# Keeping B11 + T2 apart, left operands stored one by one, half of x added by the stores, and 320 bytes in the constants

## The chip, the core and the metric

The kernel runs on one core of one Trainium2 chip. The metric is the device time of one execution in microseconds, the median of several. A profile of one further execution shows every engine: TensorE (PE) multiplies, VectorE (DVE), ScalarE (ACT) and GpSimd (POOL) work on elements, SyncE (SP) issues most transfers, POOL issues others. Sixteen DMA engines carry them all.

## What is computed

x has 2048 rows of 1024, normalised row by row to xn. One branch is linear attention with 32 heads of 32, the other a gated MLP with 3584 hidden columns; the output is x + s * silu(...). Cut to what matters:

```
xn = layernorm(x)
q, k, v = split(xn @ wqkv)                       # 32 heads of 32
s = attention(phi(q), phi(k), v) @ wo            # linear attention, first part's rest
h = silu(xn @ w1) * (xn @ w3)                    # 2048 x 3584
out = x + s * silu(h @ w2)
```

All is float32.

## The kernel before

Every large product is done by a scheme with seven products in place of eight. Two matrices are cut into 2x2 blocks; the left side gives the operands A11, A12, A22 and the sums S1 to S4, the right side B11, B21, B22 and the sums T1 to T4. The seven products are named after the right operand: B11 (with A11), T2 (S2), T3 (S3), T1 (S1), B21 (A12), T4 (A22), B22 (S4). With U = B11 + T2 the four result blocks are c11 = B11 + B21, c12 = U + T1 + B22, c21 = U + T3 + T4 and c22 = U + T3 + T1. A block A21 is needed for the sums alone. Each float32 operand is split into a high and a low half ("split", lines 82 to 84: a cast on ScalarE, a subtraction on VectorE), and each product of halves is three matmuls of 128 x 128 by 512 columns (lines 91 to 93).

The first part (to about 1700 us) makes q, k, v and the hidden h, in two halves of the rows. `hidden` (line 604) multiplies gate and up and writes h to DRAM as h_d (line 616, issued by POOL); `four_sums` lets POOL form S1 to S4, which are written as hs_d (line 624, POOL in the first half, mostly SP in the second). `divide` does the same for q and writes qs_d (line 750). The buffers of h ("sg", four) and of the sums (a pool of six) come free when the store has read them.

The second part is a row of segments (class `Segment`): attention's product with the merged wo (names ending in s), then B0 (two blocks of the hidden columns deep) and B1 to B4 (three deep). Each goes through eight groups m of 256 rows. For a group `left` (line 943) loads seven left operands (line 958, into the four sg buffers; names like rA11B), `operands` splits them one group ahead, and `tokens` (line 868) does the products and the sums. A group of three blocks is 7 x 3 x 3 = 63 matmuls.

`tokens` has two forms. The inner form (from line 908) does one product after the other in four banks a to d; catch_up lets one step of other work in between. In a segment that isn't the first, the accumulators acc[m] already hold the sums of the segments before: ScalarE copies B11 to u (911), VectorE adds T2 to u (914), and POOL then adds u to c22, c21 and c12 (917 to 919), before VectorE adds the products to them (921 to 939). The outer form (from line 881) is used in the first group of a segment and the last: all seven banks are open and k is the outer loop, so that the next segment's right operands can take the place of this one's block by block. Its sums are lines 886 to 904, with four adds on POOL (894, 897, 899, 900).

In the last segment B4 every finished block goes to `finish` (line 1006): SP loads s and x (1009, 1010), ScalarE applies silu (1011), VectorE multiplies by s and adds x (1012, 1013), POOL issues the store (1014).

A scheduler of the language orders each engine's instructions by its own model of times; engines then run in order and wait for each other by semaphores. All large tiles lie in pools behind the constants, so the constants' size sets the address of every one of them.

Of the kernel before, what the change touches and what calls it, by code (L numbers as in the profile page):

```python
# [22 lines left out]
def tile_linear_attention_times_swiglu(  # L23
# [706 lines left out]
    def divide(m, k):  # L730
# [13 lines left out]
        def steps(t):  # L744
# [5 lines left out]
            nc.gpsimd.dma_start(out=qs_d[m][:, k], in_=t)  # L750
# [87 lines left out]
    class Segment:  # L838


        def __init__(self, name, nk, first, place, right, left, acc, end=None):
# [23 lines left out]
        def add(self, e, dst, src, fresh=False):  # L865
            e.tensor_add(out=dst, in0=src, in1=dst)

        def tokens(self, m, outer, between):
# [3 lines left out]
            u = pe.tile([P, C], F32, tag="u", name=f"u{name}")  # L872
# [6 lines left out]

            if outer:  # L880
# [5 lines left out]
                nc.scalar.copy(out=u, in_=b["B11"])  # L886
                if self.first:
                    V.tensor_add(out=c11, in0=b["B21"], in1=u)
                    V.tensor_add(out=u, in0=b["T2"], in1=u)
                    V.tensor_add(out=c21, in0=b["T3"], in1=u)  # L890
                    V.tensor_add(out=c12, in0=b["T1"], in1=u)
                    V.tensor_add(out=c22, in0=b["T1"], in1=c21)
# [208 lines left out]
```

## Time and profile before

| | us |
|---|---|
| median of 3 runs | 2417.58 |
| lowest, highest | 2417.55, 2421.8 |
| profiled execution, own time | 2424.34 |
| its span, first to last instruction | 2422.6 |
| PE busy | 2343.7 (97%) |
| DVE busy | 1804.7 (74%) |
| ACT busy | 934.6 (39%) |
| POOL busy | 723.7 (30%) |
| moved by DMA | 408.62 MB |

The span is the time between the first and the last instruction of the profiled execution. Busy shares are means over stages with different limits; a stage is read by windows of time. A wait names the instruction that came last, by its engine, tile and line.

### The profile page before, as it was taken

Reading aid. Unit: us, or ns where it says so; the run is one execution under the profiler, and the core shown is the slowest. Engines: PE = TensorE matmul, PEld = TensorE weight load, DVE = VectorE, ACT = ScalarE, POOL = GpSimd, SP = SyncE. Lnnn points to the kernel's source line nnn. Section 1 sums busy time; section 2 is a strip of 40 time slices with the busy share of each in tenths; the row PEclk is TensorE's granted clock in tenths of the full one; section 3 lists DMA queues with packets and bytes.
Section 4 is the critical chain, followed back from the end, with each engine's and each line's share of the span. In section 5 each row is a group of like instructions: output and inputs, shape, how many; then the busy total and the mean of one; then the engine's idle time right before and its main releaser. Section 6 shows DMA issues by size and latency. Waiting matters only on the chain.

```text
span 2422.6 us, 30793 instructions
## 1 busy us (share of the span) xinstructions
PE 2343.7 (97%) x10544; PEld 1932.8 (80%) x10544; DVE 1804.7 (74%) x2688; ACT 934.6 (39%) x1667; POOL 723.7 (30%) x909
## 2 busy tenths in 40 slices
PE   6999999999999999999999999999899999999997
PEld 5788888777788878888878888888687887777776
DVE  8655888888787665567877887887656777776797
ACT  4434644333232234345333323334323434343443
POOL 3000112247567210000424443234330042323253
PEclk9999999999999999999999999999999999999999
DMA  3211455566567661134455555457876545453597
GB/s 125 85 52 62 152 168 167 170 199 229 198 229 238 214 228 37 51 105 139 155 187 187 198 193 188 146 185 241 252 239 200 148 124 162 119 164 114 170 289 242
DMA packets 375133, 408.62 MB, mean 169 GB/s; under 512 B 19840, under 2 KB 308608, under 8 KB 374976
## 3 DMA queue, kind: packets, MB, share of 16 engines
q1 hardware_dynamic: 348800, 319.35, 42.4%
q0 software_dynamic: 26176, 87.31, 9.6%
q8 instruction: 82, 1.34, 0.2%
q14 instruction: 75, 0.61, 0.1%
HBM read 268.96 MB, written 137.63 MB: 168 GB/s over the span
## 4 chain that ended last, share of the span: by engine, by line
PE 49%; DVE 6%; DMA 5%; issue 3%; ACT 1%; POOL 1%; DVEq 0%; SPq 0%; POOLq 0%; ACTq 0%
PE dB L91 1%; PE dB L93 1%; PE dB L92 1%; PE cB L91 1%; PE cB L93 1%; PE cB L92 1%; PE aB L93 1%; PE aB L91 1%; PE aB L92 1%; DMA rA11B<-h_d 1%; PE den L715 1%; PE kv L508 1%; DMA wpr<-wp_d 1%; PE bB L93 1%; PE bB L92 1%
## 5 line engine op out<-in xcount | busy, mean ns | idle before, releaser
L616 POOL DMA_DIRECT2D h_d<-sg x112 | 61.5, 550 | 355.5 <-DVE sg L615 352.0
L577 POOL DMA_DIRECT2D pq_d<-pq x32 | 17.5, 545 | 487.3 <-DVE pq L469 476.3
L917 POOL TENSOR_TENSOR acc<-acc,uB 128x512 f32<-128x512 f32 x25 | 41.9, 1676 | 157.9 <-DVE uB L914 157.9
L598 POOL TENSOR_TENSOR qd<-qd 128x128 f32<-128x128 f32 x32 | 25.0, 782 | 140.5 <-DVE qd L747 118.9
L894 POOL TENSOR_TENSOR acc<-acc,uB 128x512 f32<-128x512 f32 x7 | 12.0, 1710 | 145.9 <-ACT uB L886 145.9
L602 POOL TENSOR_TENSOR hs<-sg,hs 128x256 f32<-128x256 f32 x56 | 53.2, 950 | 1.5
L630 POOL TENSOR_TENSOR w<-w 128x256 f32<-128x256 f32 x28 | 26.7, 952 | 72.5 <-DMA w<-in_B_w 61.1
L1004 POOL DMA_DIRECT2D s_d<-s x32 | 17.4, 544 | 92.4 <-DVE s L924 24.5
L599 POOL TENSOR_TENSOR hs<-hs,sg 128x256 f32<-128x256 f32 x56 | 42.7, 762 | 0.0
L598 POOL TENSOR_TENSOR hs<-sg,sg 128x256 f32<-128x256 f32 x56 | 42.1, 752 | 1.0
L601 POOL TENSOR_TENSOR hs<-sg 128x256 f32<-128x256 f32 x56 | 41.9, 749 | 0.0
L91 PE MATMUL cB<-T,XA22B 128*128 128x512 f32 x87 | 35.0, 402 | 6.3 <-DVE acc L921 5.9
L83 ACT CAST XS4B<-rS4B 128x384 fp32r<-128x384 f32 (+1 forms) x40 | 19.6, 490 | 54.5 <-PE cB L93 45.9
L919 POOL TENSOR_TENSOR acc<-acc,uB 128x512 f32<-128x512 f32 x25 | 40.1, 1605 | 0.0
L84 DVE TENSOR_TENSOR XS1B<-rS1B,XS1B 128x384 fp32r<-128x384 f32 (+1 forms) x40 | 36.6, 916 | 3.7 <-ACT XS1B L83 3.6
L935 DVE TENSOR_TENSOR acc<-cB,acc 128x512 f32<-128x512 f32 x25 | 17.2, 689 | 29.6 <-PE cB L93 29.6
L83 ACT CAST XS1B<-rS1B 128x384 fp32r<-128x384 f32 (+1 forms) x40 | 19.7, 493 | 46.8 <-PE cB L93 26.5
L1011 ACT ACTIVATE acc<-acc 128x512 f32<-128x512 f32 x32 | 20.2, 633 | 43.7 <-DVE acc L924 14.8
L91 PE MATMUL aB<-B,XA12B 128*128 128x512 f32 x87 | 34.1, 392 | 2.2 <-ACT uB L911 1.6
L83 ACT CAST XS3B<-rS3B 128x384 fp32r<-128x384 f32 (+1 forms) x40 | 19.6, 491 | 43.0 <-PE bB L93 15.6
L83 ACT CAST XA11B<-rA11B 128x384 fp32r<-128x384 f32 (+1 forms) x40 | 19.7, 492 | 41.8 <-PE dB L93 28.4
L91 PE MATMUL dB<-B,XS4B 128*128 128x512 f32 x87 | 34.4, 395 | 1.2 <-DVE acc L924 1.2
(5853 smaller groups left out, 8886.9 us busy)
## 6 DMA issues: line engine op xcount, KB each, us to landing
h_d<-sg POOLq DMA_DIRECT2D x112, 256.0 KB, 3.2
qs_d<-qd POOLq DMA_DIRECT2D x32, 512.0 KB, 3.7
hs_d<-hs POOLq DMA_DIRECT2D x60, 256.0 KB, 3.9
w<-in_B_w SPq DMA_DIRECT2D x56, 256.0 KB
wt_d<-w SPq DMA_DIRECT2D x28, 512.0 KB
hs_d<-hs SPq DMA_DIRECT2D x52, 256.0 KB
pq_d<-pq POOLq DMA_DIRECT2D x32, 256.0 KB, 3.3
a_dS<-xo SPq DMA_DIRECT2D x16, 512.0 KB
```

Source lines behind the costliest of these rows:

```text
L83: nc.scalar.copy(out=hi, in_=src)
L84: return nc.vector.tensor_sub(out=lo, in0=src, in1=hi.bitcast(F32))
L91: nc.tensor.matmul(acc, lhsT=wh, rhs=ah, start=start, stop=False, skip_group_check=True)
L92: nc.tensor.matmul(acc, lhsT=wh, rhs=al, start=False, stop=False, skip_group_check=True)
L93: nc.tensor.matmul(acc, lhsT=wl, rhs=ah, start=False, stop=stop, skip_group_check=True)
L598: nc.gpsimd.tensor_add(out=s1, in0=a21, in1=a22)
L599: nc.gpsimd.tensor_sub(out=s2, in0=s1, in1=a11)
L601: nc.gpsimd.tensor_sub(out=s3, in0=a11, in1=a21)
L602: nc.gpsimd.tensor_sub(out=s4, in0=a12, in1=s2)
L616: nc.gpsimd.dma_start(out=h_d[i][2 * h + c][:, 2 * k + n], in_=sg[n, c])
L917: G.tensor_add(out=c22, in0=c22, in1=u)
L919: G.tensor_add(out=c12, in0=c12, in1=u)
```

## The change

- u is no longer added to three accumulators in each segment. It is stored to DRAM (u_d, one tile per group, issued by POOL: `keep`), loaded again by SP in the next segment with the group's left operands, and B11 and T2 of all segments are added to it, on VectorE. Only the last segment adds it to c22, c21 (inner form: VectorE) and c12 (POOL), by `close`. In B0, which has nothing to add to yet, ScalarE copies the first product into an accumulator.
- h_d, hs_d and qs_d become stores with a place for each left operand, so that a load of one operand is one run per partition (1.5 KB for three blocks, 1 KB for B0, 2 KB for q) where it was runs of 512 bytes; the stores are cut into runs of 512 bytes. A21 isn't stored.
- In groups 0 to 6 of the last segment, the blocks of the second 128 rows don't load x and don't add it: the output's rows get x by a copy in DRAM during segment B2 (`lay_x`), and the store adds to them (`accum_op`).
- An unused constant of 80 floats per partition moves all pools behind it by 320 bytes.

```diff
+    const.tile([P, 80], F32, name="gap")
...
+    LEFT = ["A11", "A12", "A22", "S1", "S2", "S3", "S4"]
+    PLACE = {"A11": (0, 1), "A12": (2, 4), "A22": (3, 5), "S1": (6, 7), "S2": (8, 9), "S3": (10, 11), "S4": (12, 13)}
+    h_d = [[dram.tile([P, 7 * NT, (f1 - f0) // 2, P], F32, name=f"h_d{f0}_{c}") for c in range(NCH)] for f0, f1 in FB]
...
+    qs_d = [dram.tile([P, 7, ND // 2, P], F32, name=f"qs_d{m}") for m in range(S // (2 * P))]
+    u_d = [dram.tile([P, C], F32, name=f"u_d{m}") for m in range(S // (2 * P))]
...
-            nc.gpsimd.dma_start(out=h_d[i][2 * h + c][:, 2 * k + n], in_=sg[n, c])
+            src = sg[n, c].rearrange("p (g t s) -> p g t s", t=2, s=P)[:, :, 0] if n == 0 else \
+                sg[n, c].rearrange("p (e s) -> p e s", s=P)
+            nc.gpsimd.dma_start(out=h_d[i][2 * h + c][:, 2 * n:4 * n + 2, k], in_=src)
...
-                queue.dma_start(out=hs_d[i][2 * h + c][:, k, e], in_=o[e])
+                queue.dma_start(out=h_d[i][2 * h + c][:, 6 + 4 * e:10 + 4 * e, k],
+                                in_=o[e].rearrange("p (e s) -> p e s", s=P))
...
-            nc.gpsimd.dma_start(out=qs_d[m][:, k], in_=t)
+            t = t.rearrange("p e (n s) -> p (e n) s", s=P)
+            nc.gpsimd.dma_start(out=qs_d[m][:, 0, k], in_=t[:, 0])
+            nc.gpsimd.dma_start(out=qs_d[m][:, 1:, k], in_=t[:, 2:])
...
+            if not self.first:
+                self.U[m] = pe.tile([P, C], F32, tag="u", name=f"u{self.name}_{m}")
+                nc.sync.dma_start(out=self.U[m], in_=u_d[m])
...
+            def more(c, src):
+                return V.tensor_add(out=c, in0=src, in1=c)
+            def take(c, src):
+                if not self.first:
+                    return more(c, src)
+                if self.last:
+                    return V.tensor_add(out=c, in0=src, in1=u)
+                return nc.scalar.copy(out=c, in_=src)
+            def close(e, c):
+                if self.last and not self.first:
+                    e.tensor_add(out=c, in0=c, in1=u)
+            def keep():
+                if not self.last:
+                    G.dma_start(out=u_d[m], in_=u)
...
-                copied = nc.scalar.copy(out=u, in_=ba)
+                copied = nc.scalar.copy(out=u, in_=ba) if self.first else more(u, ba)
...
-                added = V.tensor_add(out=u, in0=bb, in1=u)
+                added = more(u, bb)
+                keep()
...
-                if not self.first:
-                    G.tensor_add(out=c22, in0=c22, in1=u)
-                    G.tensor_add(out=c21, in0=c21, in1=u)
-                    G.tensor_add(out=c12, in0=c12, in1=u)
...
-                added = V.tensor_add(out=c22, in0=bd, in1=c22)
+                added = more(c22, bd)
+                close(V, c22)
...
+                added = take(c21, bc)
+                close(V, c21)
                 end(1, 0)
+                close(G, c12)
...
+    ADDED = NG - 1
+    def added_by_dma(m, t):
+        return m < ADDED and t == 1
...
+            nc.gpsimd.dma_start(out=out[r0:r0 + P, cols], in_=a, accum_op=ALU.add)
+    def lay_x(m):
+        for t in range(2):
+            if added_by_dma(m, t):
+                rows = slice((2 * m + t) * P, (2 * m + t + 1) * P)
+                with tc.issue_after(loads[-1].ins):
+                    nc.sync.dma_start(out=out[rows, :], in_=x[rows, :])
```

VectorE in B4, from the end of group 5 into group 6 (uB is u, cB and dB are banks with a product, acc the accumulators, XS3B and the like the low halves of group 7's left operands), before:

```order
L914 TENSOR_TENSOR uB_6_19885<-bB_6_19887,uB_6_19885 128x512
L84 TENSOR_TENSOR XS3B_7_19862<-rS3B_7_19860,XS3B_7_19862 128x384
L1013 TENSOR_TENSOR acc_15090<-acc_15090,xs_01_19842 128x512
L84 TENSOR_TENSOR XS1B_7_19867<-rS1B_7_19865,XS1B_7_19867 128x384
L921 TENSOR_TENSOR acc_15091<-cB_6_19888,acc_15091 128x512
L924 TENSOR_TENSOR acc_15091<-dB_6_19889,acc_15091 128x512
L84 TENSOR_TENSOR XA12B_7_19872<-rA12B_7_19870,XA12B_7_19872 128x384
L1012 TENSOR_TENSOR acc_15091<-acc_15091,ss_11_19934 128x512
L931 TENSOR_TENSOR acc_15091<-aB_6_19886,acc_15091 128x512
L1013 TENSOR_TENSOR acc_15091<-acc_15091,xs_11_19933 128x512
```

After:

```order
L894 TENSOR_TENSOR uB_6_19704<-bB_6_19882,uB_6_19704 128x512
L89 TENSOR_TENSOR XS3B_7_19858<-rS3B_7_19856,XS3B_7_19858 128x384
L1043 TENSOR_TENSOR acc_15112<-acc_15112,xs_01_19838 128x512
L894 TENSOR_TENSOR acc_15113<-cB_6_19883,acc_15113 128x512
L89 TENSOR_TENSOR XS1B_7_19863<-rS1B_7_19861,XS1B_7_19863 128x384
L894 TENSOR_TENSOR acc_15113<-dB_6_19884,acc_15113 128x512
L89 TENSOR_TENSOR XA12B_7_19868<-rA12B_7_19866,XA12B_7_19868 128x384
L907 TENSOR_TENSOR acc_15113<-acc_15113,uB_6_19704 128x512
L894 TENSOR_TENSOR acc_15113<-aB_6_19881,acc_15113 128x512
L1041 TENSOR_TENSOR acc_15113<-acc_15113,ss_11_19926 128x512
```

The add of u to c22 (L907) has come to VectorE behind the add of T1, and the add of x to that block is gone.

VectorE where B2's last group and B3's first meet (T_2 and B_2 are the low halves of B3's third block of right operands), before:

```order
L898 TENSOR_TENSOR uB_7_17733<-T3B_7_17736,uB_7_17733 128x512
L901 TENSOR_TENSOR acc_15092<-T1B_7_17737,acc_15092 128x512
L84 TENSOR_TENSOR B_2_17931<-rB21B_2_17929,B_2_17931 128x512
L84 TENSOR_TENSOR T_2_17936<-rT4B_2_17934,T_2_17936 128x512
L84 TENSOR_TENSOR XA22B_0_17789<-rA22B_0_17787,XA22B_0_17789 128x384
L84 TENSOR_TENSOR B_2_17941<-rB22B_2_17939,B_2_17941 128x512
L84 TENSOR_TENSOR XS4B_0_17794<-rS4B_0_17792,XS4B_0_17794 128x384
L84 TENSOR_TENSOR XA11B_1_17958<-rA11B_1_17956,XA11B_1_17958 128x384
L904 TENSOR_TENSOR acc_15092<-B22B_7_17740,acc_15092 128x512
L903 TENSOR_TENSOR acc_15092<-T4B_7_17739,acc_15092 128x512
```

After:

```order
L894 TENSOR_TENSOR acc_15114<-T1B_7_17765,acc_15114 128x512 x2
L89 TENSOR_TENSOR B_2_17961<-rB21B_2_17959,B_2_17961 128x512
L894 TENSOR_TENSOR acc_15114<-T4B_7_17767,acc_15114 128x512
L89 TENSOR_TENSOR T_2_17966<-rT4B_2_17964,T_2_17966 128x512
L89 TENSOR_TENSOR XA22B_0_17819<-rA22B_0_17817,XA22B_0_17819 128x384
L89 TENSOR_TENSOR B_2_17971<-rB22B_2_17969,B_2_17971 128x512
L89 TENSOR_TENSOR XS4B_0_17824<-rS4B_0_17822,XS4B_0_17824 128x384
L894 TENSOR_TENSOR uB_0_17790<-B11B_0_18022,uB_0_17790 128x512
L894 TENSOR_TENSOR acc_15107<-B11B_0_18022,acc_15107 128x512
L89 TENSOR_TENSOR XA11B_1_17989<-rA11B_1_17987,XA11B_1_17989 128x384
```

Both adds of T1 now stand together, T4's add comes earlier, and two adds of the new segment's B11 stand between the low halves.

POOL at the first hidden stores of the first half (sg is h, hs its sums), before:

```order
L616 DMA h_d_0_84<-sg_0_10_2774 128x512
L598 TENSOR_TENSOR hs_0_0_0_2947<-sg_0_00_2731,sg_0_10_2774 128x256
L601 TENSOR_TENSOR hs_0_0_1_2948<-sg_0_00_2731 128x256
L624 DMA hs_d_1_105<-hs_0_1_0_2914 128x512
L602 TENSOR_TENSOR hs_0_1_1_2915<-sg_0_11_2714,hs_0_1_0_2914 128x256
```

After:

```order
L624 DMA h_d_0_85<-sg_0_10_2763 128x4x128
L603 TENSOR_TENSOR hs_0_0_0_2936<-sg_0_00_2720,sg_0_10_2763 128x256
L606 TENSOR_TENSOR hs_0_0_1_2937<-sg_0_00_2720 128x256
L632 DMA h_d_1_86<-hs_0_1_0_2903 128x4x128
L607 TENSOR_TENSOR hs_0_1_1_2904<-sg_0_11_2703,hs_0_1_0_2903 128x256
```

The order is the same; each store has four pieces per partition (two for the half without A21).

## Rows read from the trace of the kernel before

**Rows 1.** The page: span, then PE's busy time and instructions.

```profile
span 2422.6 us, 30793 instructions
PE 2343.7 (97%) x10544; PEld 1932.8 (80%) x10544; DVE 1804.7 (74%) x2688; ACT 934.6 (39%) x1667; POOL 723.7 (30%) x909
```

**Rows 2.** PE's waits: who waited, for whom: total us, times, longest.

```profile
PE cB L91 <- DVE acc L921: 5.9, 6, 1.7
...
PE cs L91 <- DVE s L921: 5.1, 1, 5.1
...
PE T4B L91 <- ACT uB L886: 3.3, 3, 1.3
```

**Rows 3.** Windows: length, busy us of each engine (instructions), PEclk, DMA share, GB/s.

```profile
600.00:700.00 100.00, 96.72 (x427) 79.79 (x426) 79.90 (x93) 29.95 (x51) 60.12 (x78) 1.00 0.61 203
...
1690.00:1730.00 40.00, 32.02 (x122) 23.94 (x121) 28.47 (x37) 15.06 (x26) 12.49 (x21) 0.91 0.78 250
1845.00:1876.00 31.00, 26.27 (x106) 19.14 (x105) 24.67 (x47) 18.07 (x37) 1.08 (x2) 0.99 0.84 255
1900.00:2000.00 100.00, 100.00 (x443) 82.81 (x442) 73.73 (x123) 39.01 (x79) 24.55 (x16) 1.00 0.48 141
2050.00:2077.00 27.00, 24.21 (x103) 18.66 (x103) 24.98 (x36) 11.38 (x22) 13.28 (x10) 1.00 0.63 186
2170.00:2195.00 25.00, 21.98 (x94) 16.89 (x92) 22.49 (x33) 9.36 (x19) 12.13 (x9) 1.00 0.61 180
2288.00:2306.00 18.00, 16.00 (x68) 12.29 (x67) 17.83 (x25) 7.64 (x15) 8.27 (x6) 1.00 0.66 199
2306.00:2409.00 103.00, 96.97 (x416) 77.02 (x414) 96.40 (x146) 39.37 (x77) 52.23 (x51) 1.00 0.91 293
2409.00:2422.60 13.60, 0.06 (x1) 0.00 (x0) 4.40 (x7) 1.26 (x2) 1.62 (x3) 0.59 0.27 99
```

**Rows 4.** Timeline in B4: start us, duration us, engine, line, operation, tiles.

```profile
2386.39 0.69 DVE L1012 TENSOR_TENSOR acc<-acc,ss 128x512 f32<-128x512 f32 x1
...
2387.00 0.69 DVE L914 TENSOR_TENSOR uB<-bB,uB 128x512 f32<-128x512 f32 x1
...
2387.60 0.55 DVE L84 TENSOR_TENSOR XS3B<-rS3B,XS3B 128x384 fp32r<-128x384 f32 x1
2387.77 1.53 POOL L917 TENSOR_TENSOR acc<-acc,uB 128x512 f32<-128x512 f32 x1 [0.93 <-DVE uB L914]
...
2388.06 1.78 DVE L1013 TENSOR_TENSOR acc<-acc,xs 128x512 f32<-128x512 f32 x1
...
2389.77 1.64 DVE L84 TENSOR_TENSOR XS1B<-rS1B,XS1B 128x384 fp32r<-128x384 f32 x1
...
2391.34 0.68 DVE L921 TENSOR_TENSOR acc<-cB,acc 128x512 f32<-128x512 f32 x1
```

**Rows 5.** POOL's groups: count, busy us, mean ns, idle before and releaser.

```profile
L616 POOL DMA_DIRECT2D h_d<-sg x112 | 61.5, 550 | 355.5 <-DVE sg L615 352.0 <-DVE c21u__6706 L453 3.5
...
L917 POOL TENSOR_TENSOR acc<-acc,uB 128x512 f32<-128x512 f32 x25 | 41.9, 1676 | 157.9 <-DVE uB L914 157.9
L919 POOL TENSOR_TENSOR acc<-acc,uB 128x512 f32<-128x512 f32 x25 | 40.1, 1605 | 0.0
L918 POOL TENSOR_TENSOR acc<-acc,uB 128x512 f32<-128x512 f32 x25 | 34.3, 1373 | 0.0
...
L724 POOL DMA_DIRECT2D r_d<-r x4 | 2.0, 512 | 56.2 <-DVE r L723 56.2
```

**Rows 6.** VectorE's groups from 1870 to 2410, same columns.

```profile
L84 DVE TENSOR_TENSOR T<-rT4B,T 128x512 fp32r<-128x512 f32 x12 | 11.5, 956 | 0.0
...
L84 DVE TENSOR_TENSOR T<-rT2B,T 128x512 fp32r<-128x512 f32 x11 | 7.5, 686 | 4.9 <-ACT T L83 4.9
```

**Rows 7.** Chain that ended last: start us, us, what (here transfers).

```profile
1697.16 7.24 DMA rA11q<-qs_d
...
1716.06 7.71 DMA rS3q<-qs_d
...
2376.71 3.54 DMA rA11B<-h_d
```

More of the change, by code (lines that the diff above doesn't have):

```diff
@@ L838, in tile_linear_attention_times_swiglu, with __init__ @@
     class Segment:
-        def __init__(self, name, nk, first, place, right, left, acc, end=None):
+        def __init__(self, name, nk, first, last, place, right, left, acc, end=None):
+            self.last, self.U = last, {}
             self.name, self.nk, self.first = name, nk, first
@@ L871, in tokens @@
             c11, c12, c21, c22 = (self.acc(m, t, n) for t in range(2) for n in range(2))
-            u = pe.tile([P, C], F32, tag="u", name=f"u{name}")
+            u = pe.tile([P, C], F32, tag="u", name=f"u{name}") if self.first else self.U[m]
             ks = range(self.nk)
@@ L885, in tokens @@
                     between(k)
-                nc.scalar.copy(out=u, in_=b["B11"])
                 if self.first:
+                    nc.scalar.copy(out=u, in_=b["B11"])
                     V.tensor_add(out=c11, in0=b["B21"], in1=u)
[L889 to L892, printed above, removed]
-                else:
-                    G.tensor_add(out=c11, in0=c11, in1=u)
-                    V.tensor_add(out=c11, in0=b["B21"], in1=c11)
-                    V.tensor_add(out=u, in0=b["T2"], in1=u)
-                    G.tensor_add(out=c12, in0=c12, in1=u)
-                    V.tensor_add(out=u, in0=b["T3"], in1=u)
-                    G.tensor_add(out=c21, in0=c21, in1=u)
-                    G.tensor_add(out=c22, in0=c22, in1=u)
-                    V.tensor_add(out=c12, in0=b["T1"], in1=c12)
-                    V.tensor_add(out=c22, in0=b["T1"], in1=c22)
-                V.tensor_add(out=c21, in0=b["T4"], in1=c21)
-                V.tensor_add(out=c12, in0=b["B22"], in1=c12)
+                else:
+                    more(u, b["B11"])
+                    more(c11, b["B11"])
+                    more(c11, b["B21"])
+                more(u, b["T2"])
+                keep()
+                take(c22, b["T3"])
+                take(c21, b["T3"])
+                more(c22, b["T1"])
+                take(c12, b["T1"])
+                more(c21, b["T4"])
+                more(c12, b["B22"])
+                for c in (c22, c21, c12):
+                    close(G, c)
                 for t in range(2):
@@ L927, in tokens @@
                 self.product(ba, X, "B21", ks, False)
-                if self.first:
-                    added = V.tensor_copy(c11, ba)
-                else:
-                    added = V.tensor_add(out=c11, in0=ba, in1=c11)
+                added = V.tensor_copy(c11, ba) if self.first else more(c11, ba)
                 end(0, 0)
@@ L934, in tokens, with left @@
                 self.product(bc, X, "T4", ks, False)
-                added = V.tensor_add(out=c21, in0=bc, in1=u if self.first else c21)
+                added = take(c21, bc)
+                close(V, c21)
                 end(1, 0)
+                close(G, c12)
                 catch_up(copied, added)
                 self.product(bd, X, "B22", ks, False)
-                V.tensor_add(out=c12, in0=bd, in1=u if self.first else c12)
+                take(c12, bd)
                 end(0, 1)
-    def left(m, g, halves, sums, nk, name, first=False):
-        halves = [t.rearrange("p k (g t s) -> p k g t s", t=2, s=P) for t in halves]
-        sums = [t.rearrange("p k (n g s) -> p k n g s", n=2, s=P) for t in sums]
-        where = {"A11": halves[0][:, :, g, 0], "A12": halves[1][:, :, g, 0], "A22": halves[1][:, :, g, 1]}
-        for n in range(4):
-            where[f"S{n + 1}"] = sums[n // 2][:, :, n % 2, g]
+    loads = []
+    def left(m, src, nk, name, first=False):
         big = None
@@ L957, in left @@
                 t = signed(f"r{n}{name}_{m}")[:, :nk * P].rearrange("p (k s) -> p k s", s=P)
-            load = nc.sync.dma_start(out=t, in_=where[n])
+            loads[:] = [nc.sync.dma_start(out=t, in_=src(n))]
             if name == "q" and m < 2:
-                fetched[:] = [load]
+                fetched[:] = loads
             yield n, t
@@ L966, in queries @@
             next(jobs[0][0])
[L967 to L968 removed]
+        return left(m, lambda n: qs_d[m][:, LEFT.index(n)], ND // 2, "q", m == 0)
     def hiddens(i, m):
[L971 to L974 removed]
+        return left(m, lambda n: h_d[i][m // NT][:, PLACE[n][m % NT]], (FB[i][1] - FB[i][0]) // 2, f"B{i}")
     asked = {}
```

40 lines of the change are left out of this document (17 added, 23 removed).

## The prediction

> **What bounds the kernel now.** I read the page first. TensorE is busy for 2343.7 of 2422.6 us [rows 1], so only what stops it can be won, and the rest of the reading is to find where it stops and for whom.
>
> Next comes the list of what TensorE waited for [rows 2]. The long entries of the second part are banks that come free late: "cB" behind VectorE's add of line 921 (5.9 us in six waits), "cs" behind the same line (5.1 us in one), "T4B" behind the copy of line 886 (3.3 us). A wait is only part of a loss, so I price the stretches with the table of windows [rows 3]. Where nothing stops it, 1900 to 2000, TensorE does 443 matmuls in 100 us, 4.43 per us; I assume the same in every stretch and call length minus count/4.43 the loss. 1690 to 1730 (start of attention's products): 40 - 122/4.43 = 12.5 us, with the clock at 0.91. 1845 to 1876 (into segment B0): 7.0. 2050 to 2077, 2170 to 2195, 2288 to 2306 (into B2, B3, B4): 3.7, 3.8 and 2.6. 2306 to 2409 (B4 itself): 9.1. Together 38.7 us, and behind the last matmul 13.6 us more. That is all the change can win; the products stay as they are.
>
> In B4 VectorE is busy 96.4 of 103 us and the DMA engines are at 0.91 [rows 3]: the two bounds to watch. At the three transitions VectorE stands at 24.98 of 27, 22.49 of 25 and 17.83 of 18.
>
> **The last segment.** The timeline [rows 4] shows why VectorE is full. Start to start, a 128x512 operation takes 0.61 us (2386.39 to 2387.00) and a 128x384 one 0.46 (2387.60 to 2388.06). But when POOL's adds of lines 917 to 919 run, the operations with both inputs in SBUF take 1.71 and 1.57 us to the next start: 1.1 us too much each. The add of line 914, whose first input is a bank, is not seen stretched. A group before: 14 operations of 0.61 plus seven low halves of 0.46 = 11.8 us, plus twice 1.1 = 14.0 us, against 63/4.43 = 14.2 us of matmuls. No room, so any late operand shows on TensorE.
>
> After: the B11 add comes to VectorE (+1), two closing adds of u come (+2), two of the four adds of x go (-2): 15 operations, 9.2 + 3.2 = 12.4 us. Of POOL's three adds (1.4 to 1.7 us each) [rows 5] one stays; it can stretch one VectorE operation, so 12.4 to 13.5 us, 87 to 95% of the group. The wait of c22's first add for POOL, which the order shows behind u's second add, is gone. What is late next are the loads: a left operand takes 3.54 us to land [rows 7] with the engines at 0.91. There the change takes 14 loads of x away and brings eight loads of u, all of the same 256 KB, and 14 stores that also read what they add to. I bound the loss left between 1 and 9 us and take 4: the VectorE share of it goes, the DMA share stays. **-5 us** (0 to -8).
>
> **The transitions into B2, B3 and B4.** An outer group has ten adds on VectorE where it had seven and a copy on ScalarE, and two outer groups meet: 6 x 0.61 = +3.7 us of VectorE. Eight POOL adds per transition go (lines 894 to 900). Of what they stretched, one row shows it plainly: the low half of T4 is 956 ns, that of T2 686 [rows 6]; 12 of them over four transitions make 0.8 us each. If two operations per outer group were stretched by 1.1 us, it is 4.4. So VectorE's work changes by -0.7 to +2.9 us per transition, while the chain in which every second add waited for POOL goes, and with it the waits of cB just behind the transition (part of the 5.9 us). Gain or loss is open: I take **-2 us** for the three, with -6 and +11 (all 3.7 us paid on TensorE, three times) as ends. VectorE's queue behind the B11 adds holds the next group's low halves, and TensorE waits for those.
>
> **Into attention and B0.** Left operands come in runs of 2 KB (attention), 1 KB (B0) and 1.5 KB, where each run was 512 B. What that is worth in DMA time: 0.48 of the engines gave 141 GB/s in 1900 to 2000, mostly such loads, and 0.61 gave 203 at 600 to 700 [rows 3]: 13% more engine time per byte. At 1690 to 1730 the 14 loads of q are 3.7 MB of the stretch's 10 MB, so 13% of 37% of 0.78 x 40 us = 1.5 us; single loads take 7.24 and 7.71 us to land there [rows 7] and the 5.1 us wait hangs on one. I take **-2 us** (0 to -4). Into B0 the same sum gives 0.8 us, and the copies of c22, c21 and c12 move to ScalarE: **-0.5 us** (+1 to -1.5).
>
> **The first part.** The stores of h and its sums come in 512 B runs now: 256 or 512 pieces where there were 128; a quarter of h, A21, isn't stored. Nothing waits for the data for long, but POOL issues most of them in order ahead of its sums, and VectorE and ScalarE wait for the buffers that those free. An issue of 128 rows takes 550 ns, one of 32 rows 512 [rows 5]: 0.4 ns a piece, 0.70 us for 512. In proportion to pieces it would be 2.2 us. A pair of hidden blocks lasts 168/4.43 = 37.9 us and POOL is busy 60% of it [rows 3], 15 us free; eight issues grow from 4.4 to 15.4 us at worst. That fits, so **0**, under cover of POOL's idle time. The 32 further issues of qs_d and the 32 stores of u go under the same cover, and the seven copies of x into the output fall in B2, where the engines stand near 0.5.
>
> **The tail.** The last group's closing add of c21 stands on VectorE ahead of c12's last add: **+0.6 us**.
>
> **The gap** moves every later tile by 320 B. No row tells what an address costs: **0**. The Trainium skill, "DMA: Bandwidth & Descriptors", section "How a descriptor splits into AXI transactions", says a transfer starts on a 256 B boundary and fetches the bytes in front for nothing. Tiles at 192 past such a boundary would take 22 beats for 512 B instead of 16, an estimate from that page; by it the last segment's loads would come sooner and the loss there would be 2 us instead of 4. No run here shows it.
>
> **The sum.** -5 - 2 - 2 - 0.5 + 0.6 = -8.9 us. The profiled execution took 2424.34 us, 1.7 us more than its span [rows 1], and would take 2415.4; it lies 6.8 us over the median of 2417.58, so the median after is **2408.7 us**, -0.37%. A measurement of this kernel can tell about 0.2%, 4.8 us, from no change.
>
> **Rivals.**
> - Transitions eat the gain. VectorE is 90 to 99% full there and gets more adds. If the stretched operations save only 0.8 us, each transition costs up to 2.9 us more and the -2 turns to about +5: 2415 to 2416 us, no change.
> - The same, paid in full: the 3.7 us of every transition land on TensorE because what was stretched had room. +11 in place of -2: 2422 us, slower. It decides where the freed waits for POOL are worth under 1.3 us a transition. Against it: the waits of rows 2 name those POOL chains.
> - Accumulating stores fill the DMA engines. A 256 KB store must read 256 KB more; at twice the engine time 14 of them use what the loads of x gave back, at four times the 0.91 goes to 1 and B4 stays where it was or loses 4 more: 2414 to 2418 us, no change.
> - POOL's issues grow beyond proportion. It decides at 2.35 us an issue (15 us free over eight, plus 0.55). At 2.6 us POOL lacks 2 us a pair; over the nine or ten pairs of 500 to 860 that is 19 us: 2428 us, slower.
> - The operand loads don't get shorter, since a load of 3.5 us is mostly not its pieces. Then only the last segment and the transitions give: 2411 us.
> - The start address sets the pitch of matmuls. Rows 3 give 225.7 ns per matmul of 512 columns at the full clock; 512 columns at 2.4 GHz are 213.3 ns. If the addresses, all shifted by the gap, cause the rest, some 9,600 of the 10544 matmuls [rows 1] lose up to 12 ns each: 115 us, 2294 us. Nothing in the trace says so, as all operands have one offset. The Trainium skill, "TensorE: Matmul & The Clock Gate", section "Wait — 56ns, not 53.3ns?", gives 215.7 ns for 512 columns; by it the estimate is 96 us and 2313 us. The trace disagrees with that figure as it stands.
>
> **How the numbers follow.** Forecast 0.50, own range 2399 to 2414 (the ends of its larger terms together); transitions eat the gain 0.15; paid in full 0.10; accumulating stores 0.08; loads not shorter 0.09; POOL 0.05; pitch 0.03. Faster by over 0.2% means below 2412.7: nearly all of the forecast (0.46), the loads (0.08), the pitch (0.03) and a little of the transitions (0.03), 0.60. Slower means above 2422.4: POOL (0.05), half of the full payment (0.06) and a rest of the stores (0.03), 0.14. Between them 0.26. The range 2397 to 2423 leaves out the pitch, POOL and the outer parts of the others, under 2 in 10.
>
> **What the profile after would show.** The windows of the same stretches tell each term: the loss of B4 down to about 4 us with VectorE under 93%; no wait for the adds after T3 by POOL; no 1.1 us stretches except beside the one POOL add; the transitions between 2 and 4 us each; a q load landing in 5 to 6 us; POOL's issue of h_d at 0.6 to 0.9 us. Wrong would be: TensorE waiting for "uB" or "acc" adds of bank B11 at the transitions, DMA at 1.0 in B4, POOL over 90% at 600 to 700, a loss that moved into the first part, or another matmul pitch.

## The result, and the profile after

| | before | after |
|---|---|---|
| median, us (4 runs each) | 2419.69 | 2381.4 |
| lowest, highest | 2417.55, 2426.66 | 2380.12, 2387.55 |
| ratio, 95% interval | | 0.984 [0.981, 0.987] |
| profiled execution, span | 2424.34, 2422.6 | 2381.26, 2379.0 |

The change makes the kernel 1.6% faster, some 38 us. The forecast was 2408.7 us and its range ended at 2397: the sign was right, the size was not. The two profiled executions differ by 43 us, since the one of before was a long one.

The page after answers to [rows 1]: span, then PE's busy time and instructions.

```profile
span 2379.0 us, 30872 instructions
PE 2331.0 (98%) x10544; PEld 1928.3 (81%) x10544; DVE 1760.0 (74%) x2713; ACT 931.1 (39%) x1659; POOL 716.5 (30%) x880
```

TensorE's busy time fell by 12.7 us of 2343.7, and the pitch of its matmuls is the same (443 in 100 us, as in [rows 3]). So most of the gain is waits that went. To see where, I cut after at the same matmuls as before. Columns as in [rows 3]; first a window of before in the first part, which [rows 3] leave out:

```profile
450.00:700.00 250.00, 240.06 (x1056) 197.36 (x1055) 203.68 (x252) 80.90 (x137) 136.37 (x178) 0.99 0.61 201
```

Then after: the same matmuls, the start of attention, into B0, into B2, into B3, into B4, B4, the tail.

```profile
448.40:688.40 240.00, 238.24 (x1055) 196.09 (x1054) 197.24 (x249) 81.20 (x137) 157.15 (x178) 1.00 0.61 200
...
1670.50:1708.70 38.20, 32.24 (x122) 22.73 (x121) 27.76 (x38) 13.47 (x25) 14.61 (x18) 0.96 0.77 261
1823.80:1852.80 29.00, 24.94 (x105) 19.22 (x105) 23.02 (x43) 19.69 (x42) 2.17 (x4) 1.00 0.84 269
2025.30:2048.40 23.10, 23.10 (x103) 19.14 (x102) 21.71 (x40) 8.24 (x16) 1.08 (x2) 1.00 0.84 279
2141.40:2162.20 20.80, 20.80 (x93) 17.23 (x92) 20.37 (x37) 7.04 (x14) 1.08 (x2) 1.00 0.79 252
2255.10:2270.10 15.00, 15.00 (x67) 12.40 (x67) 15.00 (x26) 6.17 (x12) 1.57 (x2) 1.00 0.71 230
2270.10:2369.50 99.40, 96.73 (x415) 78.28 (x414) 90.85 (x150) 36.21 (x70) 34.85 (x38) 0.98 0.94 280
2369.50:2379.00 9.50, 0.40 (x2) 0.00 (x0) 5.07 (x9) 1.23 (x2) 2.03 (x4) 0.73 0.49 168
```

| stretch | before, us | after, us | won | forecast |
|---|---|---|---|---|
| to 450 of before | 450 | 448.4 | 1.6 | 0 |
| 450 to 1690 (first part) | 1240 | 1222.1 | 17.9 | 0 |
| start of attention | 40 | 38.2 | 1.8 | 2 |
| into B0 | 31 | 29.0 | 2.0 | 0.5 |
| into B2, B3, B4 | 70 | 58.9 | 11.1 | 2 |
| B4 | 103 | 99.4 | 3.6 | 5 |
| tail | 13.6 | 9.5 | 4.1 | -0.6 |
| stretches between | 475 | 473.5 | 1.5 | 0 |

Some 18 of the 43.6 us lie in the first part, for which I had put 0. Each column is one execution; a second one of the changed kernel (a_again, below), cut at the same matmuls, has 1222.7 us for the first part, 40.3 for the start of attention and 30.2 into B0.

**Where the first part stopped.** TensorE's waits of before between 100 and 1660 us:

```profile
PE cg__10225 L91 <- DVE c22g__10259 L432: 3.5, 1, 3.5
PE cg__5225 L91 <- DVE c22g__5257 L432: 3.3, 1, 3.3
PE cg__3945 L91 <- DVE c22g__3987 L432: 2.8, 1, 2.8
PE bk__7101 L93 <- DVE T2k__6953 L84: 2.1, 1, 2.1
```

Two of 2.0 and 1.9 us follow, and one of 0.9. After, two of 1.7 and 1.6 us and one of 0.4 are left. (Three waits of at most 0.5 us are in both.) Nearly all are a bank that comes free late, because VectorE is late with one add (line 432). The timeline of before ahead of the second wait (VectorE and GpSimd only) shows why it is late:

```profile
634.05 0.75 POOL L633 TENSOR_TENSOR w<-w 128x256 f32<-128x256 f32 x1
634.10 3.27 DVE L315 TENSOR_TENSOR wu__5032<-wu__5032 128x512 f32<-128x512 f32 x1
634.74 0.73 POOL L631 TENSOR_TENSOR w<-w 128x256 f32<-128x256 f32 x1
635.42 0.72 POOL L634 TENSOR_TENSOR w<-w 128x256 f32<-128x256 f32 x1
636.10 0.71 POOL L633 TENSOR_TENSOR w<-w 128x256 f32<-128x256 f32 x1
...
637.30 0.68 DVE L432 TENSOR_TENSOR c22g__5257<-cg__5225,ug__5202 128x512 f32<-128x512 f32 x1
```

A VectorE operation with two inputs in SBUF, 0.69 us elsewhere, takes 3.27: GpSimd runs four sums back to back, and VectorE's operation ends only behind the last of them. Then the add of 637.30 comes, and TensorE has lost 3.3 us. Some of the stops also cost clock: behind the one at 514 us TensorE was granted 1.2 GHz from 517.0 to 520.4, where matmuls start 0.43 us apart in place of 0.23. Two such stretches follow, from 862 and 1261 us, each behind a stop of over 2 us; after has none in the first part. At 1.6 us lost in each, an estimate from the two distances, clock (4.8 us) and waits (12.8 us less) make up 17.6 of the 17.9 us.

Counting the timeline from 200 to 1660 us, 54 VectorE operations take over 2 us before (149.7 us together), 17 after (45.3 us). Four of each count, here and in the tables below, are reciprocals, which take 3.33 us in either kernel. Of the 50 others before, 27 begin while GpSimd still issues a store, ahead of its sums. The groups of GpSimd show the other side. Before, then after, the same sum:

```profile
L601 POOL TENSOR_TENSOR hs<-sg 128x256 f32<-128x256 f32 x56 | 41.9, 749 | 0.0
```

```profile
L606 POOL TENSOR_TENSOR hs<-sg 128x256 f32<-128x256 f32 x56 | 59.6, 1064 | 0.0
```

GpSimd's sum is slower after. The two engines take turns where before VectorE was kept out.

The Trainium skill, "SBUF — State Buffer", section "Who interferes with whom", says that a VectorE instruction with two SBUF inputs contends with a GpSimd instruction that reads SBUF, under an exclusive lock. The rows agree, and show more: one such instruction can be passed over by a whole run of GpSimd's.

### The profile page after: what moved, and what is told of

It reads as the page before. It is cut to its first block, busy times and chain, and to the rows that moved or that the text cites. A ratio compares the mean times of both kernels' runs of the same rounds, so it can differ in the third digit from the quotient of the medians.

```text
span 2379.0 us, 30872 instructions
## 1 busy us (share of the span) xinstructions
PE 2331.0 (98%) x10544; PEld 1928.3 (81%) x10544; DVE 1760.0 (74%) x2713; ACT 931.1 (39%) x1659; POOL 716.5 (30%) x880
## 4 chain that ended last, share of the span: by engine, by line
PE 54%; DMA 5%; DVE 3%; issue 1%; ACT 1%; POOL 0%; SPq 0%; POOLq 0%; ACTq 0%; DVEq 0%
PE cB L96 1%; PE cB L97 1%; PE dB L97 1%; PE dB L98 1%; PE cB L98 1%; PE dB L96 1%; PE aB L97 1%; PE aB L96 1%; PE aB L98 1%; DMA rA22B<-h_d 1%; DMA wpr<-wp_d 1%; DMA rS3B<-h_d 1%; PE den L724 1%; PE bB L98 1%; PE bB L97 1%
## 5 line engine op out<-in xcount | busy, mean ns | idle before, releaser
L624 POOL DMA_DIRECT2D h_d<-sg x112 | 82.8, 740 | 287.5 <-DVE sg L620 285.7
L911 POOL DMA_DIRECT2D u_d<-uB x32 | 17.3, 541 | 406.6 <-DVE uB L894 368.4
L894 DVE TENSOR_TENSOR acc<-cB,acc 128x512 f32<-128x512 f32 x50 | 34.3, 687 | 40.6 <-PE cB L98 40.6
L894 DVE TENSOR_TENSOR acc<-dB,acc 128x512 f32<-128x512 f32 x56 | 38.5, 687 | 31.1 <-PE dB L98 30.9
L606 POOL TENSOR_TENSOR hs<-sg 128x256 f32<-128x256 f32 x56 | 59.6, 1064 | 0.0
L632 POOL DMA_DIRECT2D h_d<-hs x60 | 45.8, 765 | 4.4 <-POOL hs L607 2.7
L88 ACT CAST XA22B<-rA22B 128x384 fp32r<-128x384 f32 (+1 forms) x40 | 19.7, 492 | 48.9 <-PE aB L98 26.6
L96 PE MATMUL cB<-T,XS3B 128*128 128x512 f32 x87 | 34.2, 393 | 1.6 <-ACT XS3B L88 1.6
L96 PE MATMUL aB<-B,XA11B 128*128 128x512 f32 x87 | 34.4, 396 | 1.3 <-ACT XA11B L88 1.3
L513 PEld LDWEIGHTS kv<-kvr 128*128 128x128 f32 x256 | 33.5, 191 | 2.5
```

What stands on the lines that cost most here:

```text
L88: nc.scalar.copy(out=hi, in_=src)
L96: nc.tensor.matmul(acc, lhsT=wh, rhs=ah, start=start, stop=False, skip_group_check=True)
L513: nc.tensor.matmul(acc, lhsT=r[:, 1, t], rhs=r[:, 0, t], start=t == 0, stop=t == C // P - 1)
L606: nc.gpsimd.tensor_sub(out=s3, in0=a11, in1=a21)
L624: nc.gpsimd.dma_start(out=h_d[i][2 * h + c][:, 2 * n:4 * n + 2, k], in_=src)
L632: queue.dma_start(out=h_d[i][2 * h + c][:, 6 + 4 * e:10 + 4 * e, k], in_=o[e].rearrange("p (e s) -> p e s", s=P))
```

## Experiments

Every kernel was timed beside the kernel before; each number in brackets is the 95% interval of the ratio to it.

### The gap and the layout, each alone and each undone

b_gap adds the constant to the kernel before, a_nogap takes it out of the changed one. The order on every engine stays.

```diff
+    const.tile([P, 80], F32, name="gap")
```

> The kernel before with the gap of 320 bytes alone; the order of instructions on every engine is that of the kernel before. Theory L (the store layout spaces GpSimd's operations in the first part, and with that the 20 us won before 1695 us): the gap changes nothing, 2417 to 2421 us, and VectorE still has some 50 operations over 2 us in the first part. Theory G (the shift of all large tiles by 320 bytes changes how GpSimd and VectorE share the SBUF): most of the 20 us is won here, 2397 to 2402 us, the waits of cg for VectorE's add of line 432 shrink, and the operations over 2 us fall to under 20.

> The changed kernel without the gap; same order on every engine. Theory L: 2379 to 2384 us, as the changed kernel. Theory G: the first part is as slow as before, 2399 to 2404 us, with 50 or so VectorE operations over 2 us in it.

b_layout puts the new stores and loads of h, its sums and q, and nothing else, into the kernel before (the diff is that of the change); a_oldlayout puts the old ones into the changed kernel.

> The kernel before with the new layout of the left operands alone (stores of h, the sums and q cut into 512-byte pieces, A21 not stored, loads of one operand in one run per partition), no gap, sums of u on GpSimd as before. Theory L: the 20 us of the first part are here, together with 1 to 4 us into attention and B0: 2394 to 2400 us. Theory G: only the loads gain, 2414 to 2419 us, and the first part keeps its waits for line 432's add.

> The changed kernel with the layout of the kernel before (h, its sums and q stored as before, A21 too, operands loaded in runs of 512 bytes), the gap kept. Theory L: 2399 to 2406 us, the first part as slow as in the kernel before. Theory G: 2382 to 2387 us, the first part as quick as in the changed kernel.

| | median, us | ratio |
|---|---|---|
| b_gap | 2414.42 | 0.9967 [0.9952, 0.9981] |
| a_nogap | 2388.17 | 0.9860 [0.9843, 0.9877] |
| b_layout | 2400.99 | 0.9914 [0.9897, 0.9931] |
| a_oldlayout | 2395.61 | 0.9888 [0.9864, 0.9911] |

The layout alone is worth 21 us, undone it costs 11 to 14; VectorE's operations over 2 us are 16 or 17 with it and 54 to 56 without, whether the gap is there or not. So theory L holds for what it counts, though a_nogap and a_oldlayout took neither theory's times. Cut at the same matmuls, the 1240 us of the first part of before are 1224.6 in b_layout, 1233.7 in b_gap, 1226.2 in a_nogap and 1235.9 in a_oldlayout, against 1222.1 after. The gap is worth 8 us in the kernel before, against both theories: too much for L, too little for G, and with 56 long operations.

### The sums of u and x undone, the pieces alone, a delay alone

a_oldu has the sums of u of the kernel before, here the inner form; a_noadd loads and adds x in every block.

```diff
-copied = nc.scalar.copy(out=u, in_=ba) if self.first else more(u, ba)
+copied = nc.scalar.copy(out=u, in_=ba)
...
+if not self.first:
+    G.tensor_add(out=c22, in0=c22, in1=u)
+    G.tensor_add(out=c21, in0=c21, in1=u)
+    G.tensor_add(out=c12, in0=c12, in1=u)
```

```diff
-ADDED = NG - 1
+ADDED = 0
```

> The changed kernel with the sums of the kernel before: u copied by ScalarE and added on GpSimd in every segment, nothing of u stored or loaded; layout, gap and the accumulating stores of x kept. Theory (the second part's gain is GpSimd's adds of u leaving VectorE's path): TensorE's stops of the kernel with the new layout alone come back at the transitions into B2, B3, B4 and in B4, 47.2 - 32.3 = 14.9 us there against about 4 us in the changed kernel: 2391 to 2396 us, and up to 4 us more if these adds also make the end after the last matmul longer. Rival (the gain there came with the layout's loads or with x): 2381 to 2385 us.

> The changed kernel in which every block of the last segment loads x and adds it on VectorE as before; no copy of x into the output, no adding stores. Theory of the prediction (VectorE is the bound of B4): two more operations of 0.61 us a group, 13.6 us against 14.2 us of matmuls, so B4 loses 2 to 5 us: 2383 to 2387 us. Rival (with the adds of u off GpSimd VectorE has room anyway): 2380 to 2383 us, no change.

b_pieces cuts the stores of h and its sums into 512-byte pieces and leaves the rest:

```diff
-nc.gpsimd.dma_start(out=h_d[i][2 * h + c][:, 2 * k + n], in_=sg[n, c])
+nc.gpsimd.dma_start(out=h_d[i][2 * h + c][:, :, 2 * k + n], in_=sg[n, c].rearrange("p (e s) -> p e s", s=P))
```

> The kernel before, with h and its sums stored in runs of 512 bytes as the changed kernel does, but A21 stored too and the operands loaded in runs of 512 bytes as before; q, u, x and the constants as before. Theory S (an issue of a store that takes GpSimd 0.19 us longer shifts its sums against VectorE's operations, and with that VectorE waits less): VectorE's operations over 2 us in the first part fall from about 54 to about 17 and most of the layout's 21 us is here: 2401 to 2408 us. Rival D (the layout's gain is in the loads, or in the quarter of h that is not stored): 2418 to 2424 us.

b_delay16 leaves all stores and puts two memsets behind the store (`stored`) and ahead of the sums:

```diff
+            with tc.issue_after(stored.ins):
+                for e in range(2):
+                    nc.gpsimd.memset(o[e][:, :16], 0.0)
```

> The kernel before with two small memsets on GpSimd (128x16, some 0.1 us each, into places that the sums then overwrite) between each pair's store of h and its sums; no store or load is changed. Theory S: the 0.2 us shift GpSimd's sums as the longer issue does, 2402 to 2412 us, with the operations of VectorE over 2 us down to under 30. Rival P (it is the pieces themselves, in the DMA engines, that help): 2420 to 2426 us, with 50 or more such operations.

| | median, us | ratio | VectorE over 2 us |
|---|---|---|---|
| a_oldu | 2395.02 | 0.9904 [0.9884, 0.9924] | 17 |
| a_noadd | 2387.17 | 0.9870 [0.9853, 0.9886] | 16 |
| b_pieces | 2443.18 | 1.0093 [1.0067, 1.0118] | 59 |
| b_delay16 | 2399.80 | 0.9924 [0.9909, 0.9939] | 16 |

My theory S was half wrong. A longer issue is not what helps: b_pieces has it (733 ns for h_d) and is slower than before. (Its profiled execution took 2429.9 us, near the lowest of its ten, so its trace explains only part of that loss.) But two memsets, with no store, load or byte changed, give nearly all that the layout gives. The first part, 1240 us before, takes 1218.8 in b_delay16 and 1250.5 in b_pieces. TensorE's waits there in b_delay16, without the three short ones:

```profile
PE bk__7157 L93 <- DVE T2k__7005 L84: 0.7, 1, 0.7
PE cg__10293 L91 <- DVE c22g__10327 L432: 0.3, 1, 0.3
```

What differs is when GpSimd's sums begin. First before, at one of many like places; the add of c12u (line 461) is released by TensorE and serves as a mark:

```profile
1482.90 0.54 POOL L616 DMA_DIRECT2D h_d<-sg  x1 [2.19 <-DVE sg L615]
1483.33 0.69 DVE L461 TENSOR_TENSOR c12u__12096<-du__11978,uu__11951 128x512 f32<-128x512 f32 x1 [0.73 <-PE du__11978 L93]
1483.46 0.75 POOL L598 TENSOR_TENSOR hs<-sg,sg 128x256 f32<-128x256 f32 x1
1484.04 2.10 DVE L84 TENSOR_TENSOR B22g__12081<-wg__11796,B22g__12081 128x512 fp32r<-128x512 f32 x1
1484.16 0.74 POOL L601 TENSOR_TENSOR hs<-sg 128x256 f32<-128x256 f32 x1
1484.85 0.74 POOL L599 TENSOR_TENSOR hs<-hs,sg 128x256 f32<-128x256 f32 x1
```

The same place after:

```profile
1464.55 0.71 POOL L624 DMA_DIRECT2D h_d<-sg  x1 [0.32 <-DVE sg L620]
1464.88 0.69 DVE L466 TENSOR_TENSOR c12u__12100<-du__11981,uu__11954 128x512 f32<-128x512 f32 x1 [0.63 <-PE du__11981 L98]
1465.28 0.75 POOL L603 TENSOR_TENSOR hs<-sg,sg 128x256 f32<-128x256 f32 x1
1465.59 1.04 DVE L89 TENSOR_TENSOR B22g__12085<-wg__11797,B22g__12085 128x512 fp32r<-128x512 f32 x1
1465.97 1.24 POOL L606 TENSOR_TENSOR hs<-sg 128x256 f32<-128x256 f32 x1
1466.55 1.22 DVE L620 TENSOR_TENSOR sg<-c12u__12100,sg 128x512 f32<-128x512 f32 x1
```

And in b_delay16:

```profile
1463.23 0.69 DVE L461 TENSOR_TENSOR c12u__12186<-du__12066,uu__12039 128x512 f32<-128x512 f32 x1 [0.73 <-PE du__12066 L93]
1463.33 0.17 POOL L624 MEMSET hs<- 128x16 f32 x2
1463.55 0.73 POOL L598 TENSOR_TENSOR hs<-sg,sg 128x256 f32<-128x256 f32 x1
1463.94 0.90 DVE L84 TENSOR_TENSOR B22g__12171<-wg__11884,B22g__12171 128x512 fp32r<-128x512 f32 x1
1464.25 1.18 POOL L601 TENSOR_TENSOR hs<-sg 128x256 f32<-128x256 f32 x1
```

The first sum begins 0.13 us behind the start of c12u's add before, 0.40 after, 0.32 in b_delay16. VectorE's next operation, the low half of B22g, then starts 0.12 us ahead of GpSimd's second sum before, and is passed over by it and the next: 2.10 us. It starts 0.38 and 0.31 us ahead in the others, gets its turn when the first sum ends, and from there the two alternate at 0.9 to 1.2 us each. In b_pieces the two distances are 0.24 and 0.22 us, and the operation takes 2.28: shifted, but not far enough. The distance does not decide alone: the operation of 634.10 above began 0.64 us ahead of GpSimd's next sum and was passed over all the same.

### Which gap, and the delay put on the other kernels

b_gap16 and b_gap64 are b_gap with 16 and 64 floats. a_delay16 and ao_delay16 add the two memsets to the changed kernel and to a_oldlayout.

> The kernel before with a gap of 16 floats (64 bytes): the large tiles then start, as with 320 bytes, on a multiple of 256 bytes, where before they start 192 bytes past one. The gap of 320 bytes alone gave 2414.4 against 2422.4 us. Theory A (it is the start within 256 bytes): 0.9952 to 0.9981 of the kernel before, some 8 us. Rival C (it is chance: any small shift in times moves which VectorE operation meets a run of GpSimd's sums): a value of its own, anywhere within 8 us of the kernel before on either side, and not tied to the start.

> The kernel before with a gap of 64 floats (256 bytes): every large tile moves, but still starts 192 bytes past a multiple of 256. Theory A: no change, 0.999 to 1.001. Rival C: a value of its own, within 8 us of the kernel before on either side; a gain of 4 us or more here would speak against theory A.

> The changed kernel with the two memsets of 128x16 on GpSimd between each pair's store of h and its sums. If the first part still loses time to VectorE operations caught behind a run of sums (17 over 2 us are left; TensorE's stops at 510 and 1242 us are 1.8 us each, with 1.7 us of half clock behind one at most), up to 4 us are to be had: 2377 to 2381 us. If what counts is only where the sums fall against VectorE's operations, and the changed kernel is already in a good place, the same 0.2 us may spoil it: 2382 to 2398 us, with 30 to 55 operations over 2 us.

> The changed kernel with the layout of the kernel before (2395.6 us) and the two memsets between store and sums. Theory S (the layout's gain is the place of GpSimd's sums in time, not its loads): the first part's stops go, 2379 to 2385 us, level with the changed kernel. Rival L (a good part of the layout's 14 us is in the loads and the unstored A21): 2388 to 2396 us.

| | median, us | ratio | VectorE over 2 us |
|---|---|---|---|
| b_gap16 | 2413.34 | 0.9968 [0.9956, 0.9980] | 54 |
| b_gap64 | 2421.94 | 1.0002 [0.9987, 1.0017] | 52 |
| a_delay16 | 2381.43 | 0.9834 [0.9814, 0.9854] | 29 |
| ao_delay16 | 2381.46 | 0.9832 [0.9811, 0.9852] | 16 |

ao_delay16 loads every operand in 512-byte runs and stores A21, and is as fast as the changed kernel. Beside the memsets, the layout is worth nothing that can be measured. a_delay16 has 29 long operations and is no slower: in its first part no wait of TensorE is over 0.6 us. So the time hangs on those few long operations that TensorE waits for, not on their number. ao_delay16's window of the first part has no stop left, 237.10 us busy of 237.10:

```profile
448.40:685.50 237.10, 237.10 (x1055) 196.41 (x1054) 190.24 (x248) 81.56 (x137) 145.84 (x202) 1.00 0.62 209
```

The gap is a matter of where tiles start: 64 bytes give what 320 give, 256 bytes, which leave the start within 256 bytes as it was, give nothing. The window 450 to 700 us, by matmuls done: before 1056 (above); then b_gap, b_gap16, b_gap64:

```profile
450.00:700.00 250.00, 244.19 (x1081) 200.61 (x1080) 207.83 (x256) 82.24 (x139) 140.23 (x184) 1.00 0.62 206
450.00:700.00 250.00, 246.19 (x1084) 202.68 (x1083) 206.82 (x256) 82.44 (x139) 141.74 (x185) 0.99 0.62 208
450.00:700.00 250.00, 241.29 (x1055) 198.31 (x1055) 203.61 (x252) 81.72 (x138) 138.52 (x178) 0.99 0.61 202
```

What moves with the start is the time of GpSimd's queue on the DMA engines. Its 26,176 packets take 9.6% of the engines' time before and in b_gap64, 9.3% in b_gap and b_gap16; in the first part one of 4096 bytes takes 165 ns (median) in the first two and 159 in the others. A store of h lands after 3.2 us before, 3.1 in b_gap64, 2.9 in b_gap and 3.0 in b_gap16. The rule of the Trainium skill that the prediction weighed ("DMA: Bandwidth & Descriptors", section "How a descriptor splits into AXI transactions") points the right way here, but not as I used it: the packets of 512 bytes of the second part's loads take 27 ns (median) at either start. How a slightly shorter store saves 8 us is not settled; the gain sits in the first part's waits for line 432, 14.4 us before, 9.9 in b_gap and 8.1 in b_gap16.

### u, x and the size of the delay once more

a_again is the changed kernel again and a_noadd_b is a_noadd again, both on one chip; ao_delay_oldu is ao_delay16 with the old sums of u; b_delay8 has eight memsets in place of two.

> The changed kernel once more, to stand beside the same kernel without the adding stores on the same chip: 0.983 to 0.985 of the kernel before.

> The changed kernel with x loaded and added on VectorE in every block, once more. If x is worth what the prediction put into the last segment, 2 to 5 us over a_again. If the 5.8 us seen before came from the first part (its profile lost 4 us there, where no instruction differs), 0 to 2 us over a_again.

> The changed kernel with the layout of before, the two memsets between store and sums, and the sums of u on GpSimd as before: it differs from ao_delay16 (2381.5 us) by the part of u alone, and from b_delay16 (2399.8 us) by the gap and x. By TensorE's stops the part of u is worth 8 to 14 us: 2389 to 2395 us. If u is worth little with the first part quiet: 2381 to 2385 us.

> The kernel before with eight memsets of 128x16 between store and sums in place of two (some 0.4 us in place of 0.1). Theory S (only the moment at which the sums begin counts): a value of its own between 2397 and 2425 us, with a number of VectorE operations over 2 us that goes with it. Rival M (a memset breaks up the run of GpSimd's sums or frees VectorE by itself): as good as two or better, 2392 to 2401 us, with 16 or fewer such operations.

| | median, us | ratio |
|---|---|---|
| a_again | 2387.62 | 0.9864 [0.9842, 0.9886] |
| a_noadd_b | 2389.13 | 0.9868 [0.9846, 0.9890] |
| ao_delay_oldu | 2396.34 | 0.9898 [0.9878, 0.9918] |
| b_delay8 | 2402.91 | 0.9926 [0.9905, 0.9946] |

The changed kernel missed what I expected of it: 0.9864, not 0.983 to 0.985. Its two timings lie some 5 us apart, with intervals that overlap. So a_nogap (0.9860) and a_noadd (0.9870) can't be told from the changed kernel, and a_oldlayout and a_oldu, 11 and 15 us slower than its first timing, are 6 and 10 us slower than its second.

**x** is worth nothing that can be told (0.9864 against 0.9868). B4 and the tail, a_again, then a_noadd_b:

```profile
2274.70:2374.60 99.90, 96.13 (x416) 76.90 (x414) 92.18 (x151) 36.84 (x71) 35.38 (x38) 1.00 0.93 278
2374.60:2384.10 9.50, 0.34 (x2) 0.00 (x0) 4.99 (x9) 1.23 (x2) 1.97 (x4) 0.69 0.46 165
```

```profile
2273.10:2371.40 98.30, 96.01 (x415) 78.47 (x414) 97.27 (x161) 36.27 (x69) 28.87 (x37) 0.98 0.91 308
2371.40:2383.30 11.90, 0.40 (x2) 0.00 (x0) 7.03 (x12) 1.86 (x3) 2.55 (x5) 0.72 0.65 234
```

With all of x on VectorE it is busy 97.27 of 98.3 us, and B4 is no longer for it; only the tail is, by 2.4 us.

**u** is worth 0.66% with the first part quiet, 15 to 16 us (2396.3 against 2381.5). By stretches of the two traces, old sums less new: into B2 26.9 less 23.1, into B3 24.0 less 20.9, into B4 17.6 less 15.0, B4 103.1 less 102.0, tail 13.0 less 8.1: 15.5 us in all. The two were timed on different chips, so the stretches weigh more than the medians; the same stretches of a_oldu less those of after make 12.7 us.

**The delay.** Eight memsets are as good as two, with 25 long operations against 16, so the time does not tell S from M. The trace speaks against M: at one of the places where b_delay16 still loses, the memsets run and free nothing.

```profile
1548.43 3.71 DVE L84 TENSOR_TENSOR T4g__12807<-wg__12534,T4g__12807 128x512 fp32r<-128x512 f32 x1 [0.64 <-ACT T4g__12807 L83]
1548.64 0.17 POOL L624 MEMSET hs<- 128x16 f32 x2
1548.76 0.76 POOL L602 TENSOR_TENSOR hs<-sg,hs 128x256 f32<-128x256 f32 x1
```

And in a_delay16 the same memsets raise the long operations from 17 to 29. So their effect hangs on what stands beside them. It remains a reading: no run moved the sums alone by a chosen time.

## Why the prediction was wrong, step by step

**What can be won: the first failure.** "Together 38.7 us, and behind the last matmul 13.6 us more. That is all the change can win" counted stretches from 1690 us on. The view of waits behind [rows 2] also held the waits for line 432's add, up to 3.5 us each, and I left them out because the change has no arithmetic there. Of the 43.6 us between the two traces 19.5 lie ahead of 1690.

**First part, 0 under cover of GpSimd's idle time: the term that failed.** The issue was priced well: 0.70 us estimated for 512 pieces; measured were 0.71 for 256 and 0.77 for 512, a mean of 0.74. The fault is in "cover". That GpSimd has 15 us free in a pair says that GpSimd will be done in time; it says nothing of which VectorE operation meets its sums. I priced that meeting for B4 (1.1 us) and did not look for it in the first part, where the order of POOL has GpSimd's sums right behind the stores whose issues I let grow. Its price is not 1.1 us, but up to a whole run. A shift of 0.2 us can move it either way, as b_pieces and b_delay16 show; which way, no row before the change tells.

**Transitions, -2 us: undersized, -11.1 measured**, of which ao_delay_oldu and ao_delay16 give 9.5 to u. The mechanism was right, also in sign: GpSimd's adds go and VectorE gets more adds. The size came from the mean of 956 ns in [rows 6]. The timeline of before into B2 shows what that mean hides:

```profile
2053.85 1.40 DVE L84 TENSOR_TENSOR B<-rB21B,B 128x512 fp32r<-128x512 f32 x1
2055.18 1.75 DVE L84 TENSOR_TENSOR T<-rT4B,T 128x512 fp32r<-128x512 f32 x1
2056.85 1.65 DVE L84 TENSOR_TENSOR XA22B<-rA22B,XA22B 128x384 fp32r<-128x384 f32 x1
```

Three low halves in a row are stretched by 2.9 us together (start to start), beside three GpSimd adds of 1.30 to 1.74 us. VectorE does 36 operations in 24.98 us there before [rows 3] and 40 in 21.71 after: 24.98 + 4 x 0.61 - 21.71 = 5.7 us saved, where I allowed 0.8 to 4.4. The rivals that let the transitions eat the gain fell with that: after, TensorE is busy all of 23.10, 20.80 and 15.00 us.

**B4, -5 us: 3.6, within its bounds, but not by its sum.** The loss left is 99.4 - 415/4.43 = 5.7 us, where I took 4. I charged VectorE's fullness; a_noadd_b shows it 99% busy and no slower. ao_delay_oldu and ao_delay16 differ there by 1.1 us only.

**Attention, -2 us: 1.8 measured, for a reason that fell.** ao_delay16, with the old 512-byte loads, does that stretch in 34.5 us, less than the 38.2 after, and a_again, the changed kernel itself, takes 40.3. So the agreement is luck: traces of one kernel differ there by as much as I forecast. "The operand loads don't get shorter" was right as far as the time goes. Into B0 2.0 came in place of 0.5; a_again has 30.2 us there against 29.0, and no run tells why.

**Tail, +0.6 us: -4.1 measured.** The adds behind the last matmul cost about what I said. What went is the time between GpSimd's last store and the end; see below.

**The gap, 0: some 8 us, -0.3%, in the kernel before.** In the changed one the first part tells of 4 us, the medians of nothing certain. No row of before tells what an address costs, and the one chance I gave it was a matmul pitch, which stayed.

**The other rivals.** Adding stores did not fill the DMA engines beyond 0.94 in B4 (0.97 in ao_delay16). GpSimd's issues of 512 pieces took 0.77 us, far less than in proportion to the pieces (2.2).

By the runs the parts are worth: layout 21 us in the kernel before and 6 to 14 in the changed one, u 10 to 16, the gap 8 us before and less in the changed kernel, x none. Where the memsets' shift is there, the layout adds nothing.

## What to carry to other kernels

List every stop of the engine that bounds the kernel, over the whole span, before deciding which of them a change can touch; a step without arithmetic in a stage still moves that stage's timing. Where VectorE operations with two SBUF inputs run beside chains of GpSimd operations, read the longest ones in the timeline rather than a group's mean: a chain can cost VectorE as much as it is long, and a small shift in when the two start can decide whether it does. Before a layout is credited with a gain, try a small delay at the same place: here two memsets of 0.17 us together did the work of a new layout.

## What the runs showed of the chip that I had not expected

- A VectorE operation with two SBUF inputs that starts shortly ahead of GpSimd's next operation of a run can be passed over by all of it (5.80 us in the trace of before at 1247 us, 5.96 in that of b_pieces). Where GpSimd neither computes nor issues a store as it starts, such an operation of the first part took at most 0.70 us in 17 of the 18 traces and 1.32 in the other (a_noadd_b).
- Tiles that start on a multiple of 256 bytes in place of 192 bytes past one: 0.9967 and 0.9968 (b_gap and b_gap16; 1.0002 where the start stays 192 past, b_gap64), with the same order on every engine.
- Between the end of GpSimd's last issue and the end of the span lie 8.1 us before and 3.5 us after, with nothing on TensorE, VectorE or ScalarE. The last issues, before, then after:

```profile
2413.92 0.54 POOL L1014 DMA_DIRECT2D out<-acc  x1 [0.97 <-DVE acc L1013]
```

```profile
2374.35 1.14 POOL L1044 DMA_DIRECT2D out<-acc  x2 [2.67 <-DVE acc L1043]
```

  It is 8.1 us in b_gap, b_delay16 and ao_delay_oldu, 6.4 in b_layout, 3.5 in b_pieces and 3.3 in ao_delay16: in these runs it goes with the stores that GpSimd has issued over the whole kernel, their number and pieces, not with the work at the end. It is also 4.9 us of what u is worth. What GpSimd does there stays open.
